# Linear attention with ELU features: first k loaded ahead of first q, new orders of issue, and rows of v, kv and z on multiples of 16 bytes

## The chip, the cores and the metric

The kernel runs on one core of a Trainium2 chip. The metric is the device time of one execution in microseconds (us). The profile is of a single execution, and its span (first to last instruction) is about 1.3 us shorter than the time of the same execution.

## The reference, cut to what matters

```python
# q, k, v: (1, 32, 2048, 128), bfloat16, normal numbers times 0.05
phi_q = jnp.where(q > 0, q + 1, jnp.exp(q)) + 1e-6
phi_k = jnp.where(k > 0, k + 1, jnp.exp(k)) + 1e-6
kv  = jnp.einsum("bhsd,bhse->bhde", phi_k, v)     # 128 x 128 a head
z   = jnp.einsum("bhsd->bhd", phi_k)
num = jnp.einsum("bhqd,bhde->bhqe", phi_q, kv)
den = jnp.einsum("bhqd,bhd->bhq", phi_q, z)[..., None] + 1e-6
return num / den
```

There are 32 heads of 2048 rows. The kernel splits phi(x) into min(exp(x), 1) + 1e-6 and max(x, 0) and gives both parts to TensorE. A column of ones beside v yields z with kv, in 129 columns.

## The kernel before

Every operation has a name and a list of operations that it waits for; a table holds the order of names on each engine. The parts that the change touches:

```python
NI, NO, NE, NR, NV, NQ, NK = 7, 12, 2, 2, 2, 2, 2      # buffers: loads, stores, em, rk, v1, q parts, kv
...
    NC = D + 1
    NW = D + 2
...
        v1_sb = sb([P, NV, NT, NW])          # rows of 130 bf16: v, a one, and one spare
        kvs_sb = sb([P, NK, NC])             # two buffers of 129 bf16
...
            # kv: 16 row blocks, each with min(exp) and with relu, all added into one place of PSUM
                    for j in range(a, b):
                        for part, src in ((0, em_sb[:, h % NE]), (1, rk_sb[:, h % NR])):
                            ins = e.matmul(kv_ps, lhsT=src[:, j], rhs=v1_sb[:, h % NV, j, 0:NC],
                                           start=(j + part == 0), stop=(j == NT - 1 and part == 1))
...
            # T: transposes of q; they overwrite what eq, rqa and rqb of the head before read
                add("PE", f"T{h}.{i}", g, over("ldq", h, ld_parts, a, b) + ["ident"] + ((every("eq", h - 1, q_parts) + rqs(h - 1)) if h else []))
...
            # n: for each of 16 row blocks the two parts of q against kv and z
                            e.matmul(to, lhsT=emq_sb[:, h % NQ, t], rhs=kvs_sb[:, h % NK], start=False, stop=False,
                                     skip_group_check=True)
                            ins = e.matmul(to, lhsT=rq_sb[:, h % NQ, t], rhs=kvs_sb[:, h % NK], start=False, stop=True,
                                           skip_group_check=True)
```

The loads (`ldq`, `ldk`, `ldv`) and stores (`st`) of 512 KB each are issued from one queue, in the order of a list. Each buffer has its own semaphore.

## Time and profile before

| | before |
|---|---|
| time, median of the first 3 runs | 170.4 us |
| span of the profiled run | 168.3 us |
| data moved | 67.12 MB |
| start of T4, from where a head takes 4.725 us | 27.48 us |
| start of T27 and of T31 (the last transposes) | 136.15 and 155.05 us |
| landing of q27, of k31, of q31 | 133.17, 148.15, 153.13 us |
| issue and landing of the last store | 165.89 and 168.30 us |

### The profile page before, as it was taken

The page shows a single profiled execution, that of the slowest core. Times are in us where ns is not written, and L with a number is a line of the kernel's source. Part 1 is how long each engine was busy: PE and PEld are TensorE (multiplying, and loading weights), DVE is VectorE, ACT ScalarE, POOL GpSimd, SP SyncE. Part 2 cuts the span into 40 slices and gives each one's busy share as a digit, 9 for nine tenths or more (in the row PEclk, how much of TensorE's full clock was granted, in tenths as well). Part 3 has the DMA queues.
Part 4 walks back from the last instruction along what each step waited for, and adds up shares of the span by engine and source line. Part 5 has one row for each costly group of instructions (what it writes and reads, how often), then busy time and mean ns, then how long its engine had stood idle before and what let it go on. Part 6 is the DMA issues. An engine that isn't in the chain of part 4 may idle for free.

```text
span 168.3 us, 6310 instructions
## 1 busy us (share of the span) xinstructions
PE 159.4 (95%) x2775; PEld 154.1 (92%) x2775; DVE 153.8 (91%) x267; ACT 153.7 (91%) x133; POOL 87.1 (52%) x71
## 2 busy tenths in 40 slices
PE   6999789999999999999999999999999999999960
PEld 2679779999999999999999999999999999999950
DVE  0177999999999999999999999999999999999894
ACT  3699989999999999999999999999999999998710
POOL 1436925556655555556555566556655565445000
PEclk9999999999999999999999999999999999999997
DMA  5999999999999999999999999999999999999986
GB/s 195 383 416 420 404 407 409 410 407 409 416 409 412 416 413 417 417 414 422 407 418 413 414 420 413 412 419 414 419 416 420 413 415 420 412 416 417 395 332 253
DMA packets 18748, 67.53 MB, mean 401 GB/s; under 512 B 2080, under 2 KB 2464, under 8 KB 18720
## 3 DMA queue, kind: packets, MB, share of 16 engines
q1 hardware_dynamic: 18720, 67.12, 98.9%
q8 instruction: 22, 0.36, 0.8%
q14 instruction: 6, 0.05, 0.1%
HBM read 50.33 MB, written 16.78 MB: 399 GB/s over the span
## 4 chain that ended last, share of the span: by engine, by line
PE 85%; DVE 8%; ACT 4%; issue 1%; POOL 0%; POOLq 0%
PE la L357 32%; PE la L394 18%; PE la L396 16%; PE la L368 16%; DVE la L410 4%; ACT la L336 2%; PE la L315 2%; DVE la L342 1%; DVE la L339 1%; ACT la L372 1%; PE la L389 1%; DVE la L403 1%; DVE la L381 1%; ACT la L378 1%; POOL la L301 0%
## 5 line engine op out<-in xcount | busy, mean ns | idle before, releaser
L410 DVE TENSOR_TENSOR la<-la 128x1536 bf16<-128x1536 f32 (+2 forms) x65 | 77.6, 1195 | 0.2
L396 PE MATMUL la<-la 128*128 128x129 bf16 x512 | 68.1, 220 | 0.0
L394 PE MATMUL la<-la 128*128 128x129 bf16 x512 | 68.0, 219 | 0.0
L372 ACT ACTIVATE la<-la 128x2048 bf16<-128x2048 bf16 (+2 forms) x35 | 60.3, 1732 | 5.7 <-PE la L368 3.8
L357 PE MATMUL la<-la 128*128 128x129 bf16 x1024 | 64.0, 219 | 0.7 <-DVE la L339 0.7
L350 POOL COPY la<-la 128x1024 int32<-128x1024 int32 (+1 forms) x33 | 41.9, 1273 | 38.1 <-DVE la L403 28.8
L336 ACT ACTIVATE la<-la 128x2048 bf16<-128x2048 bf16 (+1 forms) x33 | 61.4, 1863 | 0.0
L357 PEld LDWEIGHTS la<-la 128*128 128x128 bf16 x1024 | 60.0, 97 | 1.2 <-DVE la L339 0.8
L346 POOL TENSOR_SCALAR la<-la 128x1024 bf16<-128x1024 bf16 x32 | 44.5, 1393 | 29.1 <-DVE la L410 25.0
L396 PEld LDWEIGHTS la<-la 128*128 128x128 bf16 x512 | 49.5, 97 | 0.0
L394 PEld LDWEIGHTS la<-la 128*128 128x128 bf16 x512 | 47.1, 97 | 0.0
L368 PE MATMUL la<-la 128*128 128x128 bf16 x512 | 34.3, 221 | 0.4 <-DVE la L381 0.4
L389 PE MATMUL la<-la 128*128 128x3 bf16 (+1 forms) x192 | 32.3, 168 | 2.3 <-DVE la L410 1.6
L378 ACT ACTIVATE la<-la 128x1024 bf16<-128x1024 bf16 (+1 forms) x32 | 33.6, 1049 | 0.0
L368 PEld LDWEIGHTS la<-la 128*128 128x128 bf16 x512 | 29.9, 99 | 1.3 <-DVE la L381 0.5
L339 DVE TENSOR_SCALAR la<-la 128x2048 bf16<-128x2048 bf16 (+1 forms) x33 | 23.0, 696 | 3.6 <-ACT la L336 3.6
L389 PEld LDWEIGHTS la<-la 128*128 128x128 bf16 x192 | 18.7, 97 | 3.1 <-DVE la L410 2.0
L342 DVE TENSOR_SCALAR la<-la 128x1024 bf16<-128x1024 bf16 x32 | 17.1, 535 | 4.6 <-DMA la<-in_k_dram 4.6
L374 DVE TENSOR_SCALAR la<-la 128x2048 bf16<-128x2048 bf16 (+2 forms) x35 | 20.9, 599 | 0.3 <-ACT la L372 0.3
L381 DVE TENSOR_SCALAR la<-la 128x1024 bf16<-128x1024 bf16 x31 | 20.8, 671 | 0.0
L403 DVE RECIPROCAL la<-la 128x12 f32<-128x12 f32 (+2 forms) x65 | 12.8, 197 | 2.5 <-PE la L396 1.3
L362 ACT ACTIVATE la<-la 128x129 bf16<-128x129 f32 x32 | 9.1, 283 | 0.4 <-PE la L357 0.4
(14 smaller groups left out, 11.7 us busy)
## 6 DMA issues: line engine op xcount, KB each, us to landing
la<-in_q_dram SPq DMA_DIRECT2D x32, 512.0 KB, 15.5
la<-in_k_dram SPq DMA_DIRECT2D x32, 512.0 KB, 15.3
la<-in_v_dram SPq DMA_DIRECT2D x32, 512.0 KB, 15.3
out_dram<-la SPq DMA_DIRECT2D x31, 512.0 KB, 15.2
out_dram<-la SPq DMA_DIRECT2D x2, 192.0 KB, 2.5
out_dram<-la SPq DMA_DIRECT2D x1, 128.0 KB, 2.4
```

Source lines behind the costliest of these rows:

```text
L336: add("ACT", f"ek{h}.{i}", lambda e, a=a, b=b: e.activation(em_sb[:, h % NE, a:b], k_sb[:, h % NI, a:b], ACT.Exp), over("ldk", h, ld_parts ...
L339: add("DVE", f"em{h}.{i}", lambda e, a=a, b=b: e.tensor_scalar(em_sb[:, h % NE, a:b], em_sb[:, h % NE, a:b], 1.0, EPS, op0=ALU.min, op1=AL ...
L346: add("POOL", f"rkp{h}.{i}", lambda e, a=a, b=b: e.tensor_scalar(rk_sb[:, h % NR, a:b], k_sb[:, h % NI, a:b], BIG, 0.0, op0=ALU.min, op1=A ...
L350: add("POOL", f"v1{h}.{i}", lambda e, a=a, b=b: e.tensor_copy(v1_sb[:, h % NV, a:b, 0:D].bitcast(i32), v_sb[:, h % NI, a:b].bitcast(i32)), ...
L357: ins = e.matmul(kv_ps, lhsT=src[:, j], rhs=v1_sb[:, h % NV, j, 0:NC], start=(j + part == 0), stop=(j == NT - 1 and part == 1))
L368: ins = e.transpose(xT[:, j], q_sb[:, h % NI, j], ident[:])
L372: add("ACT", f"eq{h}.{i}", lambda e, a=a, b=b: e.activation(emq_sb[:, h % NQ, a:b], xT[:, a:b], ACT.Exp), over("T", h, t_parts, a, b) + fr ...
L378: add("ACT", f"rqa{h}", lambda e: e.activation(rq_sb[:, h % NQ, 0:n], xT[:, 0:n], ACT.Relu), over("T", h, t_parts, 0, n) + freed(NQ, h, (" ...
L389: e.matmul(_ap(o_ps[:, :], o + D, [[NC, m]]), lhsT=ones[:], rhs=epsr[:, 0:m], start=True, stop=False, skip_group_check=True)
L394: e.matmul(to, lhsT=emq_sb[:, h % NQ, t], rhs=kvs_sb[:, h % NK], start=False, stop=False, skip_group_check=True)
L396: ins = e.matmul(to, lhsT=rq_sb[:, h % NQ, t], rhs=kvs_sb[:, h % NK], start=False, stop=True, skip_group_check=True)
L410: return e.tensor_tensor(out=_ap(o_sb[:, :, :, :], first(o_sb[:, h % NO, t0, 0:1]) - first(o_sb[:, :, :, :]), [[m * D, nb], [D, m], [1, D] ...
```

## The change

The intent has two parts. First, with k loaded first, ScalarE can begin with exponentials of k, without waiting for transposes of q. The orders on all engines and of all loads and stores were drawn anew for that. Second, with rows of 272 bytes in place of 260, and buffers of 272 in place of 258, every row that TensorE streams starts at a multiple of 16 bytes.

```diff
-        w2 w1 T0.0 T0.1 w0 kv0.0 kv0.1 T1.0 n0.0 kv1.0 kv1.1 T2.0 n0.1 n1.0 kv2.0 kv2.1 T3.0 n1.1 kv3.0 kv3.1 n2.0
+        w1 w2 T0.1 T0.0 w0 T1.0 kv0.0 kv0.1 kv1.0 kv1.1 n0.0 n0.1 T2.0 kv2.0 kv2.1 n1.0 T3.0 n1.1 kv3.0 kv3.1 n2.0
 (TensorE: the rest as before; VectorE, ScalarE, GpSimd: new at both ends, VectorE in part of the middle too; cut)
-        ldq0.0 ldk0.0 ldv0.0 ldk1.0 ldq1.0 ldv1.0 ldk2.0 ldq2.0 ldk3.0 ldv2.0 ldv3.0 ldk4.0 ldq3.0 ldv4.0 ldq4.0
+        ldk0.0 ldq0.0 ldk1.0 ldv0.0 ldq1.0 ldv1.0 ldk2.0 ldk3.0 ldv2.0 ldq2.0 ldv3.0 ldq3.0 ldk4.0 ldv4.0 ldk5.0
 (queue: another order of loads and stores to the end; cut)
-    NW = D + 2
+    NW = D + 8
-        kvs_sb = sb([P, NK, NC])
+        kvs_sb = sb([P, NK, NW])
-            add("DVE", f"v1ones{s}", lambda g, s=s: g.memset(v1_sb[:, s, :, D:NW], 1.0))
+            add("DVE", f"v1ones{s}", lambda g, s=s: g.memset(v1_sb[:, s, :, D:D + 2], 1.0))
 (kvs_sb is then written and read as kvs_sb[:, h % NK, 0:NC], in three places; cut)
```

More of the change, by code (lines that the diff above doesn't have):

```diff
@@ L96 @@
     "DVE": """
-        v1ones0 rkd0.0 em0.0 eps0 em0.1 v1ones1 emq0.0 rqb0.0 emq0.1 eps1 rkd1.0 eps2 ones em1.0 r0.0 rqb1.0 f0.0
-        emq1.0 rkd2.0 em2.0 rkd3.0 em3.0 rqb2.0 r1.0 rkd4.0 r0.1 f0.1 emq2.0 f1.0 em4.0 rqb3.0 r1.1 rkd5.0 f1.1 r2.0
-        emq3.0 f2.0 em5.0 rqb4.0 r2.1 rkd6.0 f2.1 r3.0 emq4.0 f3.0 em6.0 rqb5.0 r3.1 rkd7.0 f3.1 r4.0 emq5.0 f4.0
-        em7.0 rqb6.0 r4.1 rkd8.0 f4.1 r5.0 emq6.0 f5.0 em8.0 rqb7.0 r5.1 rkd9.0 f5.1 r6.0 emq7.0 f6.0 em9.0 rqb8.0
-        r6.1 rkd10.0 f6.1 r7.0 emq8.0 f7.0 em10.0 r7.1 rqb9.0 f7.1 rkd11.0 r8.0 emq9.0 f8.0 em11.0 r8.1 rqb10.0 f8.1
@@ L102 @@
-        emq10.0 r9.0 rkd12.0 f9.0 em12.0 rqb11.0 r9.1 rkd13.0 f9.1 r10.0 emq11.0 f10.0 em13.0 r10.1 rqb12.0 f10.1
-        rkd14.0 r11.0 emq12.0 f11.0 em14.0 rqb13.0 r11.1 rkd15.0 f11.1 r12.0 emq13.0 f12.0 em15.0 r12.1 rqb14.0
-        f12.1 emq14.0 r13.0 rkd16.0 f13.0 em16.0 rqb15.0 r13.1 rkd17.0 f13.1 r14.0 emq15.0 f14.0 em17.0 rqb16.0
-        r14.1 rkd18.0 f14.1 r15.0 emq16.0 f15.0 em18.0 rqb17.0 r15.1 rkd19.0 f15.1 r16.0 emq17.0 f16.0 em19.0
-        rqb18.0 r16.1 f16.1 rkd20.0 r17.0 emq18.0 f17.0 em20.0 rqb19.0 r17.1 f17.1 rkd21.0 r18.0 emq19.0 f18.0
@@ L107 @@
-        em21.0 r18.1 rqb20.0 f18.1 rkd22.0 r19.0 emq20.0 f19.0 em22.0 r19.1 rqb21.0 f19.1 rkd23.0 r20.0 emq21.0
-        f20.0 em23.0 rqb22.0 r20.1 rkd24.0 f20.1 r21.0 emq22.0 f21.0 em24.0 rqb23.0 r21.1 rkd25.0 f21.1 r22.0
-        emq23.0 f22.0 em25.0 rqb24.0 r22.1 rkd26.0 f22.1 r23.0 emq24.0 f23.0 em26.0 rqb25.0 r23.1 rkd27.0 f23.1
-        r24.0 emq25.0 f24.0 em27.0 r24.1 rqb26.0 f24.1 r25.0 rkd28.0 emq26.0 f25.0 em28.0 r25.1 rqb27.0 f25.1
-        emq27.0 r26.0 rkd29.0 f26.0 em29.0 r26.1 rqb28.0 f26.1 emq28.0 r27.0 rkd30.0 f27.0 em30.0 rqb29.0 r27.1
@@ L112 @@
-        rkd31.0 f27.1 r28.0 emq29.0 f28.0 em31.0 r28.1 rqb30.0 f28.1 r29.0 emq30.0 f29.0 emq31.0 emq31.2 r29.1
-        emq31.1 f29.1 r30.0 f30.0 r30.1 f30.1 r31.0 f31.0 r31.1 r31.2 f31.1 f31.2
+        eps0 ones rkd0.0 v1ones1 v1ones0 eps2 rkd1.0 em0.0 rqb0.0 emq0.0 emq0.1 em0.1 em1.0 rqb1.0 rkd2.0 eps1
+        emq1.0 rkd3.0 r0.0 em2.0 f0.0 em3.0 rqb2.0 r0.1 emq2.0 f0.1 r1.0 rkd4.0 f1.0 em4.0 rqb3.0 r1.1 rkd5.0 f1.1
+        r2.0 emq3.0 f2.0 em5.0 rqb4.0 r2.1 rkd6.0 f2.1 r3.0 emq4.0 f3.0 em6.0 rqb5.0 r3.1 rkd7.0 f3.1 r4.0 emq5.0
@@ new lines @@
+        f4.0 em7.0 rqb6.0 r4.1 rkd8.0 f4.1 r5.0 emq6.0 f5.0 em8.0 rqb7.0 r5.1 rkd9.0 f5.1 r6.0 emq7.0 f6.0 em9.0
+        rqb8.0 r6.1 rkd10.0 f6.1 r7.0 emq8.0 f7.0 em10.0 rqb9.0 r7.1 rkd11.0 f7.1 r8.0 emq9.0 f8.0 em11.0 r8.1
+        rqb10.0 f8.1 emq10.0 r9.0 rkd12.0 f9.0 em12.0 r9.1 rqb11.0 f9.1 emq11.0 r10.0 rkd13.0 f10.0 em13.0 rqb12.0
+        r10.1 rkd14.0 f10.1 r11.0 emq12.0 f11.0 em14.0 rqb13.0 r11.1 rkd15.0 f11.1 r12.0 emq13.0 f12.0 em15.0
+        rqb14.0 r12.1 rkd16.0 f12.1 r13.0 emq14.0 f13.0 em16.0 rqb15.0 r13.1 rkd17.0 f13.1 r14.0 emq15.0 f14.0
@@ new lines @@
+        em17.0 rqb16.0 r14.1 rkd18.0 f14.1 r15.0 emq16.0 f15.0 em18.0 rqb17.0 r15.1 rkd19.0 f15.1 r16.0 emq17.0
+        f16.0 em19.0 rqb18.0 r16.1 f16.1 rkd20.0 r17.0 emq18.0 f17.0 em20.0 rqb19.0 r17.1 f17.1 emq19.0 r18.0
+        rkd21.0 f18.0 em21.0 r18.1 rqb20.0 f18.1 rkd22.0 r19.0 emq20.0 f19.0 em22.0 r19.1 rqb21.0 f19.1 emq21.0
+        r20.0 rkd23.0 f20.0 em23.0 r20.1 rqb22.0 f20.1 emq22.0 r21.0 rkd24.0 f21.0 em24.0 r21.1 rqb23.0 f21.1
+        emq23.0 r22.0 rkd25.0 f22.0 em25.0 rqb24.0 r22.1 rkd26.0 f22.1 r23.0 emq24.0 f23.0 em26.0 rqb25.0 r23.1
@@ L114 @@
+        rkd27.0 f23.1 r24.0 emq25.0 f24.0 em27.0 r24.1 rqb26.0 f24.1 emq26.0 r25.0 rkd28.0 f25.0 em28.0 r25.1
+        rqb27.0 f25.1 emq27.0 r26.0 rkd29.0 f26.0 em29.0 rqb28.0 r26.1 f26.1 r27.0 rkd30.0 emq28.0 f27.0 em30.0
+        rqb29.0 r27.1 rkd31.0 f27.1 r28.0 emq29.0 f28.0 em31.0 rqb30.0 r28.1 f28.1 r29.0 emq30.0 f29.0 emq31.1
+        emq31.0 r29.1 f29.1 r30.0 f30.0 r30.1 f30.1 emq31.2 r31.0 f31.0 r31.1 r31.2 f31.1 f31.2
     """,
     "ACT": """
-        eq0.0 eq0.1 ek0.0 ek0.1 rqa0 ek1.0 kvs0 eq1.0 rqa1 ek2.0 kvs1 ek3.0 eq2.0 rqa2 kvs2 ek4.0 eq3.0 kvs3 rqa3
+        ek0.0 ek0.1 eq0.1 eq0.0 rqa0 ek1.0 eq1.0 kvs0 ek2.0 rqa1 kvs1 ek3.0 eq2.0 kvs2 rqa2 ek4.0 eq3.0 kvs3 rqa3
@@ L122 @@
         ek26.0 eq25.0 kvs25 rqa25 ek27.0 eq26.0 kvs26 rqa26 ek28.0 eq27.0 kvs27 rqa27 ek29.0 eq28.0 kvs28 rqa28
-        ek30.0 eq29.0 kvs29 rqa29 ek31.0 eq30.0 kvs30 rqa30 eq31.2 eq31.0 eq31.1 kvs31 rqa31
+        ek30.0 eq29.0 kvs29 rqa29 ek31.0 eq30.0 kvs30 rqa30 eq31.1 eq31.0 kvs31 eq31.2 rqa31
     """,
     "POOL": """
-        ident0 ident rkp0.0 v10.0 v10.1 v11.0 rkp1.0 rkp2.0 v12.0 rkp3.0 v13.0 v14.0 rkp4.0 v15.0 rkp5.0 v16.0
+        ident0 ident v10.0 rkp0.0 v10.1 rkp1.0 v11.0 rkp2.0 v12.0 v13.0 rkp3.0 v14.0 rkp4.0 v15.0 rkp5.0 v16.0
         rkp6.0 v17.0 rkp7.0 v18.0 rkp8.0 v19.0 rkp9.0 v110.0 rkp10.0 v111.0 rkp11.0 v112.0 rkp12.0 v113.0 rkp13.0
@@ L132 @@
     "SP": """
-        ldq0.0 ldk0.0 ldv0.0 ldk1.0 ldq1.0 ldv1.0 ldk2.0 ldq2.0 ldk3.0 ldv2.0 ldv3.0 ldk4.0 ldq3.0 ldv4.0 ldq4.0
-        ldk5.0 ldv5.0 ldk6.0 ldq5.0 ldv6.0 ldv7.0 ldk7.0 ldq6.0 ldk8.0 ldq7.0 ldk9.0 ldk10.0 ldq8.0 ldv8.0 ldv9.0
-        ldq9.0 st0.0 ldq10.0 ldq11.0 ldq12.0 st1.0 ldv10.0 ldk11.0 ldk12.0 ldv11.0 st2.0 ldv12.0 ldq13.0 ldk13.0
-        ldv13.0 st3.0 ldk14.0 ldk15.0 st4.0 ldv14.0 ldv15.0 ldq14.0 ldk16.0 st5.0 ldk17.0 ldq15.0 ldv16.0 ldv17.0
-        st6.0 ldq16.0 ldq17.0 ldv18.0 ldk18.0 ldv19.0 ldv20.0 st7.0 ldq18.0 ldk19.0 st8.0 ldk20.0 ldk21.0 ldq19.0
-        ldk22.0 ldk23.0 st9.0 ldq20.0 ldv21.0 st10.0 ldq21.0 ldv22.0 ldk24.0 ldq22.0 st11.0 ldq23.0 ldv23.0 st12.0
-        ldv24.0 ldk25.0 ldk26.0 ldq24.0 st13.0 ldq25.0 ldv25.0 ldv26.0 st14.0 ldk27.0 ldq26.0 st15.0 ldv27.0 ldq27.0
-        ldk28.0 st16.0 ldv28.0 ldq28.0 ldk29.0 st17.0 ldv29.0 ldk30.0 ldq29.0 ldv30.0 st18.0 ldk31.0 ldq30.0 st19.0
+        ldk0.0 ldq0.0 ldk1.0 ldv0.0 ldq1.0 ldv1.0 ldk2.0 ldk3.0 ldv2.0 ldq2.0 ldv3.0 ldq3.0 ldk4.0 ldv4.0 ldk5.0
+        ldq4.0 ldv5.0 ldk6.0 ldq5.0 ldq6.0 ldv6.0 ldk7.0 ldq7.0 ldk8.0 st0.0 ldv7.0 ldv8.0 ldv9.0 ldk9.0 ldk10.0
+        ldq8.0 ldk11.0 ldq9.0 st1.0 ldv10.0 ldq10.0 ldq11.0 ldk12.0 ldk13.0 ldv11.0 ldv12.0 ldq12.0 st2.0 ldv13.0
+        ldk14.0 ldk15.0 ldv14.0 ldq13.0 ldq14.0 st3.0 ldq15.0 ldq16.0 ldk16.0 ldv15.0 ldq17.0 st4.0 ldv16.0 ldk17.0
+        ldq18.0 st5.0 ldk18.0 ldv17.0 ldk19.0 st6.0 ldv18.0 ldk20.0 ldv19.0 ldv20.0 st7.0 ldk21.0 ldq19.0 ldk22.0
+        st8.0 ldv21.0 ldq20.0 ldv22.0 st9.0 ldq21.0 ldq22.0 ldk23.0 ldk24.0 st10.0 ldv23.0 ldq23.0 st11.0 ldv24.0
+        ldk25.0 ldq24.0 st12.0 ldq25.0 ldq26.0 ldv25.0 st13.0 ldk26.0 ldv26.0 st14.0 ldk27.0 ldk28.0 ldv27.0 ldv28.0
+        st15.0 ldq27.0 ldk29.0 st16.0 ldq28.0 ldv29.0 ldq29.0 ldk30.0 st17.0 ldq30.0 ldv30.0 st18.0 ldk31.0 st19.0
         ldv31.0 ldq31.0 st20.0 st21.0 st22.0 st23.0 st24.0 st25.0 st26.0 st27.0 st28.0 st29.0 st30.0 st31.0 st31.1
@@ L361, in head @@
                     + [f"v1ones{h % NV}"] + ([f"kvs{h - 1}"] if h else []) + (fs(h - 3, [5]) if h >= 3 else []))
-            add("ACT", f"kvs{h}", lambda e: e.activation(kvs_sb[:, h % NK], kv_ps, ACT.Copy),
+            add("ACT", f"kvs{h}", lambda e: e.activation(kvs_sb[:, h % NK, 0:NC], kv_ps, ACT.Copy),
                 every("kv", h, kv_parts) + freed(NK, h, ("n", groups)))
@@ L393, in g @@
                             to = o_ps[:, o + NC * c:o + NC * (c + 1)]
-                            e.matmul(to, lhsT=emq_sb[:, h % NQ, t], rhs=kvs_sb[:, h % NK], start=False, stop=False,
+                            e.matmul(to, lhsT=emq_sb[:, h % NQ, t], rhs=kvs_sb[:, h % NK, 0:NC], start=False, stop=False,
                                      skip_group_check=True)
-                            ins = e.matmul(to, lhsT=rq_sb[:, h % NQ, t], rhs=kvs_sb[:, h % NK], start=False, stop=True,
+                            ins = e.matmul(to, lhsT=rq_sb[:, h % NQ, t], rhs=kvs_sb[:, h % NK, 0:NC], start=False, stop=True,
                                            skip_group_check=True)
```

## The prediction

> **What bounds the kernel now.** Names first. Each of 32 heads has these pieces: `ek`, `eq` (exponentials on ScalarE), `em`, `emq` (min and add on VectorE), `rkd`, `rqb` (relu on VectorE), `rkp` and `v1` (relu and copy of v on GpSimd), and on TensorE `T` (16 transposes of q), `kv` (32 matmuls into kv and z), `n` (32 matmuls for the output, in two groups n.0 and n.1). ScalarE then also has `kvs` (kv out of PSUM) and `rqa` (relu of half of q); VectorE has `r` (reciprocal) and `f` (the product that is stored). I read the page first, part by part:
>
> ```profile
> PE 159.4 (95%) x2775; PEld 154.1 (92%) x2775; DVE 153.8 (91%) x267; ACT 153.7 (91%) x133; POOL 87.1 (52%) x71
> DMA  5999999999999999999999999999999999999986
> GB/s 195 383 416 420 404 407 409 410 407 409 416 409 412 416 413 417 417 414 422 407 418 413 414 420 413 412 419 414 419 416 420 413 415 420 412 416 417 395 332 253
> q1 hardware_dynamic: 18720, 67.12, 98.9%
> ```
>
> Four resources are near full, so no share alone names the bound. Transfers: 67.12 MB at the 413 GB/s of the middle slices is 162.5 us; from the first bytes at about 2.2 us that gives 164.7, and with the last receipts some 166, against a span of 168.3. Only the last three slices show slack: 395, 332 and 253 against 413 are 259 GB/s short over 4.2 us each, 1.1 MB or 2.6 us. So **no reordering of compute can win more than about 2 us**.
>
> Then the timeline, for one steady head (ScalarE, then TensorE, whose matmuls of one kind are merged):
>
> ```profile
> 26.18 0.28 ACT L362 ACTIVATE la<-la 128x129 bf16<-128x129 f32 x1
> 26.36 1.02 ACT L378 ACTIVATE la<-la 128x1024 bf16<-128x1024 bf16 x1
> 27.26 1.91 ACT L336 ACTIVATE la<-la 128x2048 bf16<-128x2048 bf16 x1
> 29.07 1.88 ACT L372 ACTIVATE la<-la 128x2048 bf16<-128x2048 bf16 x1
> ```
> ```profile
> 24.15 2.00 PE L357 MATMUL la<-la 128*128 128x129 bf16 x32
> 25.99 0.17 PE L389 MATMUL la<-la 128*128 128x3 bf16 x1
> ...
> 27.48 1.05 PE L368 MATMUL la<-la 128*128 128x128 bf16 x16
> 28.37 0.17 PE L389 MATMUL la<-la 128*128 128x2 bf16 x1
> ```
>
> A loop closes here: kv (24.15 to 26.15) releases kvs at 26.18; kvs and rqa run to 27.38; T starts 0.10 later at 27.48, since it overwrites what rqa reads; n.1 follows at 28.37 and the next kv at 28.87. That is 4.72 us, and T comes every 4.725 us from 27.48 to 155.05. ScalarE has a reserve: its other instructions start 104 ns before the previous one's recorded end, kvs only 40 ns, so it waits about 64 ns a head.
>
> VectorE in the same stretch:
>
> ```profile
> 28.86 1.74 DVE L410 TENSOR_TENSOR la<-la 128x1536 bf16<-128x1536 f32 x1
> 30.52 0.68 DVE L339 TENSOR_SCALAR la<-la 128x2048 bf16<-128x2048 bf16 x1
> 31.11 0.68 DVE L381 TENSOR_SCALAR la<-la 128x1024 bf16<-128x1024 bf16 x1
> 31.72 0.17 DVE L403 RECIPROCAL la<-la 128x4 f32<-128x4 f32 x1
> 31.81 0.57 DVE L342 TENSOR_SCALAR la<-la 128x1024 bf16<-128x1024 bf16 x1
> 32.29 0.68 DVE L410 TENSOR_TENSOR la<-la 128x512 bf16<-128x512 f32 x1
> 32.89 0.21 DVE L403 RECIPROCAL la<-la 128x12 f32<-128x12 f32 x1
> 33.03 0.62 DVE L374 TENSOR_SCALAR la<-la 128x2048 bf16<-128x2048 bf16 x1
> 33.58 1.74 DVE L410 TENSOR_TENSOR la<-la 128x1536 bf16<-128x1536 f32 x1
> ```
>
> From f to f it is 4.72 us with no gap. So in a head with this order VectorE is as full as the loop. Where r.1 stands before rqb the trace shows a wait of about 170 ns for n.1: those heads can go faster.
>
> **What the Trainium skill says.** "SBUF — State Buffer", Specifications (TRN2): SBUF has 16-byte lines, and each access that crosses to a new line pays. The trace agrees in part. Rows of v beside ones are 260 bytes, so row j lies 0, 4, 8 or 12 bytes off a line in turn. In the single records, the first matmul on a row takes, start to start, 56.0, 60.9, 59.4 and 59.5 ns for these four, the second one on the same row 56 throughout. "TensorE: Matmul & The Clock Gate", Wait — 56ns, not 53.3ns?: N/2.4 GHz plus about 2.5 ns, an estimate of 55.8 ns for 128 columns and 56.3 for 129; the trace has 55.6 for T and 56.2 for n, and 57.5 for kv. "SBUF — State Buffer", SBUF: two separate sides: VectorE in its two-port modes and GpSimd exclude each other for whole instructions. It agrees: rkd takes 0.57 us beside GpSimd and 0.36 away from it. "DMA: Bandwidth & Descriptors", Where 436 GB/s comes from: a ceiling of 435 GB/s; the trace holds 404 to 422, so the transfers can't go faster.
>
> **Alignment.** With rows of 272 bytes every row starts on a line. Saved per head: 4 rows of each kind times (4.9 + 3.4 + 3.5) ns = 47 ns of kv. kv and z of odd heads lie 2 bytes off today: their n matmuls take 56.4 and 56.2 ns against 56.05 and 56.0 of even heads, 16 x 0.4 + 16 x 0.2 = 10 ns a head on half of the heads. The loop is 4.725 us; kv lies in it whole, so it would fall to about 4.675, for which ScalarE's 64 ns suffice. Times 31 heads: 1.5 us. But 15 of the 28 steady heads keep the VectorE order shown, 4.72 us without a gap, both before and after the change; n.0 needs the previous f.0, and has only some 0.05 us of slack there (f ends at 30.59, n.0 starts at 30.71). So these win nearly nothing, and the other 13 up to 50 ns: **0.65 us**, not 1.5. ScalarE's kvs takes the same 175 ns to the next start in either slot, so nothing there.
>
> **First k ahead of first q.** Loads land in the order of issue, 1.25 to 1.3 us apart, so I put the new order on the old landing times: k0 4.2, q0 5.4, k1 7.7, v0 9.0, q1 10.25, v1 11.5, q2 16.7, q3 19.7. ScalarE starts with ek at 4.3 instead of eq at 5.8, and is through rqa0 at 9.4 instead of 10.5. T1 now stands before kv0: T1 at 10.3, kv0 at 11.3 (before 9.35), kv1 at 13.6 behind v1's copy (before 14.1), n0 15.4 to 17.4, T2 17.4 (before 15.95), kv2 18.3 (before 20.03, where it had waited for em2, and T3 for rqb2), n1.0 20.1, rqa2 until 21.6, T3 21.7 (before 22.40), kv3 23.1, T4 26.5 against 27.48. Head: **1.0 us** won, an estimate good to 0.5. Compute alone: 1.0 + 0.65 = 1.65 us.
>
> **The transfers take most of it back.** The queue is saturated from 3 us until 159 us, so the n-th transfer lands when it did before, whatever compute does. I gave each load of the new order the landing time of its place and compared with its first use before. Most loads have 1 to 10 us to spare. Three don't: q27 moves two places back and lands at 135.73, with T27 at 136.15: 0.42 us to spare. k31 moves from place 112 to 113, lands at 149.39, and ek31 was at 150.11: 0.7 us. v31 stays at 151.88, as now just in time for GpSimd:
>
> ```profile
> 152.00 1.04 POOL L350 COPY la<-la 128x1024 int32<-128x1024 int32 x1 [1.77 <-DMA la<-in_v_dram]
> ```
>
> but its copy is needed only by kv31 at 156.45. So at T27 at most 0.4 us of the 1.5 won survives; the last four heads may add 4 x 0.05, under the 0.7 us that k31 allows: 0.6 at T31. kv31 and the last n add 0.05 to 0.1. The order of the tail (eq31 parts, one emq31 part later) I take for neutral, since the tail is kv31, n30.0, f30.0, n31, f31 as before. Sum: **0.7 us** off 170.4, that is 169.7.
>
> **Rivals.** (1) Loop alone: alignment counts in every head (1.5) and the head too (1.0): 2.5 us, cut to about 1.8 by the transfers' floor, 168.6. For it: no wait on VectorE shows on TensorE in mid-kernel today. Against: f's gapless 4.72 us and the landing of q27. (2) VectorE and transfers hide everything: 170.3. For it: q27's place; against: it has 0.4 us to spare, and the end has free bandwidth. (3) The new head is worse: kv0 starts two us later, since v0 is now fourth; if em2 or a GpSimd copy then runs late, T4 doesn't gain, and late loads cost besides: 170.8. Against: between T1 and T4 the old head loses 2.1 us to waits (16.3 us where three heads are 14.2), and these the new order largely avoids.
>
> **Range and chances.** The floor by transfers gives 168.6, the three runs of before spread by 0.5, a bad head gives 170.8. I take 168.7 to 170.5. Over 2% faster would be 167.0 or less, below the floor: 0.02. Slower by 2% needs 3.4 us of new waits: 0.01.
>
> **What would show it.** kv of a head should take 1.79 us instead of 1.84, with all first matmuls on a row at 56 ns. T4 should start near 26.5. The pitch of T should stay about 4.72 where VectorE has the gapless order and fall to 4.67 elsewhere. T27 should wait for q27's landing near 135.7, and ek31 start just behind k31. T31 should start near 154.4. It is wrong if loads land earlier by place than before (then up to 168.6), if gapless VectorE heads shorten, for instance because GpSimd's work falls elsewhere, or if the head is upset by a wait that I don't see.

## More of the kernel before

One more line of the page is needed later, the share of the engines in the chain that ended last. It is followed back from the last instruction (the last product on VectorE, not the landing of the last store), at each step to what released it:

```profile
PE 85%; DVE 8%; ACT 4%; issue 1%; POOL 0%; POOLq 0%
```

No transfer stands in it. By this chain the end is set by TensorE, and a shorter TensorE ought to help.

## The result, and the profile after

| | before | after |
|---|---|---|
| time, median of 6 runs | 170.34 us (170.03 to 170.61) | 169.93 us (169.53 to 170.39) |
| ratio, 95% interval | | 0.9977 (0.9958 to 0.9996) |
| ratio in a second session (6 runs, 11 of before) | | 0.9996 (0.9966 to 1.0026) |
| T4 | 27.48 | 27.02 |
| T26 | 131.43 | 130.50 |
| T27 | 136.15 | 136.19 |
| T31 | 155.05 | 154.99 |
| issue and landing of the last store | 165.89, 168.30 | 165.79, 168.51 |

A ratio is the mean time of one kernel's runs over that of the other's of the same rounds, so not quite the ratio of the medians. The verdict is "same": 0.4 us in the first session, and a second session that can't tell the kernels apart.

The first lines of the page, the rates of transfer by slice, and the chain that ended last, of the changed kernel:

```profile
PE 158.2 (94%) x2775; PEld 152.7 (91%) x2775; DVE 153.9 (91%) x267; ACT 153.6 (91%) x133; POOL 85.3 (51%) x71
GB/s 207 380 420 410 411 406 409 406 419 410 405 412 409 416 406 411 416 411 418 413 415 418 413 422 411 410 419 414 417 415 416 417 415 420 413 416 416 389 331 237
...
PE 76%; DMA 14%; DVE 3%; POOL 3%; SPq 1%; issue 1%
PE la L357 30%; PE la L394 17%; PE la L368 15%; PE la L396 15%; DMA la<-in_q_dram 10%; DMA la<-in_v_dram 4%; DVE la L410 3%; POOL la L350 2%; POOL la L346 1%; SPq L324 1%; PE la L389 1%; DVE la L403 0%; DVE la L374 0%
```

TensorE is busy for 1.2 us less, so matmuls did get shorter. The rates in the middle are as before, and so is the dip in the last three slices. New is that transfers hold 14% of the chain that ended last, most of it loads of q.

The timeline of one steady head on TensorE after the change (to be held against the lines of kv, n and T in the prediction):

```profile
27.02 1.05 PE L368 MATMUL la<-la 128*128 128x128 bf16 x16
...
28.41 1.98 PE L357 MATMUL la<-la 128*128 128x129 bf16 x32
30.23 0.17 PE L389 MATMUL la<-la 128*128 128x3 bf16 x1
...
31.72 1.05 PE L368 MATMUL la<-la 128*128 128x128 bf16 x16
```

From kv to the n behind it are 1.82 us instead of 1.84, and T follows T after 4.70 us instead of 4.72. Alignment is worth 25 ns a head.

Then T27, first in the kernel before, then in the changed one:

```profile
135.76 0.17 PE L389 MATMUL la<-la 128*128 128x3 bf16 x1
136.15 1.05 PE L368 MATMUL la<-la 128*128 128x128 bf16 x16
```
```profile
134.83 0.17 PE L389 MATMUL la<-la 128*128 128x3 bf16 x1
136.19 1.05 PE L368 MATMUL la<-la 128*128 128x128 bf16 x16 [0.83 <-DMA la<-in_q_dram]
```

The last part of n before T27 starts 0.93 us earlier after the change, and T27 starts 0.04 us later: it waits 0.83 us for its load of q. The pitch from T26 to T27 is 5.69 us instead of 4.70. One wait takes away all that had been won since the start.

The head of the changed kernel on TensorE and on GpSimd:

```profile
10.32 1.05 PE L368 MATMUL la<-la 128*128 128x128 bf16 x16 [0.47 <-DVE la L374]
11.22 1.98 PE L357 MATMUL la<-la 128*128 128x129 bf16 x32
14.35 1.97 PE L357 MATMUL la<-la 128*128 128x129 bf16 x32 [1.15 <-POOL la L350]
```
```profile
8.99 0.86 POOL L350 COPY la<-la 128x512 int32<-128x512 int32 x1 [7.52 <-DMA la<-in_v_dram]
9.82 1.21 POOL L346 TENSOR_SCALAR la<-la 128x1024 bf16<-128x1024 bf16 x1
10.98 0.80 POOL L350 COPY la<-la 128x512 int32<-128x512 int32 x1
11.74 1.48 POOL L346 TENSOR_SCALAR la<-la 128x1024 bf16<-128x1024 bf16 x1
13.17 1.03 POOL L350 COPY la<-la 128x1024 int32<-128x1024 int32 x1
```

T1 and kv0 start as predicted (at 10.32 and 11.22, where 10.3 and 11.3 were expected). kv1 waits for the copy of v1, which stands fifth on GpSimd and ends at 14.20. Of the four pieces ahead of it the two half copies take longer than in the old head, 0.86 and 0.80 us instead of 0.61 and 0.62; the two relus take 1.21 and 1.48, about what they took there (1.28 and 1.47).

### The profile page after: what moved, and what is told of

Its sections match the earlier page's. It is cut to its first block, busy times and chain, and to the rows that moved or that the text cites. A ratio compares the mean times of both kernels' runs of the same rounds, so it can differ in the third digit from the quotient of the medians.

```text
span 168.6 us, 6305 instructions
## 1 busy us (share of the span) xinstructions
PE 158.2 (94%) x2775; PEld 152.7 (91%) x2775; DVE 153.9 (91%) x267; ACT 153.6 (91%) x133; POOL 85.3 (51%) x71
## 3 DMA queue, kind: packets, MB, share of 16 engines
q1 hardware_dynamic: 18720, 67.12, 98.9%
## 4 chain that ended last, share of the span: by engine, by line
PE 76%; DMA 14%; DVE 3%; POOL 3%; SPq 1%; issue 1%
PE la L357 30%; PE la L394 17%; PE la L368 15%; PE la L396 15%; DMA la<-in_q_dram 10%; DMA la<-in_v_dram 4%; DVE la L410 3%; POOL la L350 2%; POOL la L346 1%; SPq L324 1%; PE la L389 1%; DVE la L403 0%; DVE la L374 0%
## 5 line engine op out<-in xcount | busy, mean ns | idle before, releaser
L350 POOL COPY la<-la 128x1024 int32<-128x1024 int32 (+1 forms) x33 | 39.9, 1209 | 46.2 <-DVE la L403 29.6
L374 DVE TENSOR_SCALAR la<-la 128x2048 bf16<-128x2048 bf16 (+2 forms) x35 | 22.4, 641 | 0.1
L381 DVE TENSOR_SCALAR la<-la 128x1024 bf16<-128x1024 bf16 x31 | 21.0, 679 | 1.5 <-ACT la L372 1.3
L342 DVE TENSOR_SCALAR la<-la 128x1024 bf16<-128x1024 bf16 x32 | 14.9, 467 | 6.5 <-DMA la<-in_k_dram 6.0
```

The lines of the kernel that those rows point to most:

```text
L350: add("POOL", f"v1{h}.{i}", lambda e, a=a, b=b: e.tensor_copy(v1_sb[:, h % NV, a:b, 0:D].bitcast(i32), v_sb[:, h % NI, a:b].bitcast(i32)), ...
```

## The experiments

Two theories stood against each other. **Q**: the place of q27 in the queue takes the gain back, so mending it gives the gain. **F**: the transfers have a floor close to the present time, so no compute shows in it. Kernels of one call ran on the same chip and share the runs of before.

**The parts apart.** `align_only` has the old orders with the new rows and buffers; `order_only` has the new orders with the old rows:

```diff
 align_only = before with
-    NW = D + 2
+    NW = D + 8          (and kvs_sb of NW, its uses cut to 0:NC; ones written into two columns only)
 order_only = after with these taken back
```

> The old orders, with only the rows of v and the buffers of kv and z on multiples of 16 bytes. Both theories: the second and third rows of kv lose their 59 to 61 ns, kv takes 1.757 us from first to last start (as in the changed kernel) and the pitch of T falls from 4.725 to 4.70, so that compute is 27 x 0.025 = 0.65 us ahead at T31. Theory Q (the place of q27 in the queue is what takes the gain back): the old load order has no such late load (the closest is q30 with 0.94 us to spare), so the time falls by 0.5 to 0.7 us, ratio 0.996 to 0.997. Theory F (the slowest of the 16 transfer engines sets the end, whatever compute does): the time falls by under 0.2 us, ratio over 0.9985.

> The new orders, with the old rows of 260 bytes and buffers of 258. Both theories: T4 near 27.0 (0.46 us earlier than before), pitch of T 4.725, T26 0.4 us earlier than before. Theory Q: T27 waits for q27 near 136.0, where compute would have been at 135.7, so the gain is gone and the time is that of before, ratio 0.999 to 1.001. Theory F: the same, ratio 0.999 to 1.001; if it shows 0.997 the gain of the change comes from the order of the transfers themselves.

`align_only`: 170.09 against 170.36, ratio 0.9989 (0.9962 to 1.0016); this interval holds what each of the two theories expected, so the time decides nothing here. kv takes 1.757 us from first to last start, as expected. At T24 compute is 0.29 us ahead (121.69 against 121.98). But T31 starts at 155.22, later than before. The loads of this execution landed later than in the trace of before, v25 at 124.19 instead of 123.00, where GpSimd had had 0.12 us to spare. GpSimd's copy and relu then fall on top of VectorE's em25, which takes 1.11 us instead of 0.68:

```profile
124.32 1.04 POOL L350 COPY la<-la 128x1024 int32<-128x1024 int32 x1 [2.67 <-DMA la<-in_v_dram]
124.79 1.11 DVE L339 TENSOR_SCALAR la<-la 128x2048 bf16<-128x2048 bf16 x1
```

T25 and T26 come after 4.86 and 5.00 us; the same happens at v31 and em31 (1.05 us). So in this execution of the old order too the lead is lost to a load, by way of GpSimd. That I had not expected.

`order_only`: 170.38, ratio 1.0 (0.9973 to 1.0028), T27 waits for q27 (landed 136.40) as expected. Wrong was T4: 27.45, no gain at all. Repeats below put the head of the new order at 27.46, 27.13 and 27.12, so against the one trace of before **the head is worth 0 to 0.5 us, not 1.0**. The old head varies as much: T4 of the other kernels with the old orders comes between 27.21 (`pitch264`) and 28.42 (`pitch512`), so single traces can't size this gain.

**The late loads mended.** In the changed kernel, q27 goes two places and k31 one place forward:

```diff
-ldv27.0 ldv28.0 st15.0 ldq27.0 ldk29.0 ... ldv30.0 st18.0 ldk31.0 st19.0
+ldv27.0 ldq27.0 ldv28.0 st15.0 ldk29.0 ... ldv30.0 ldk31.0 st18.0 st19.0
```

> The changed kernel with first-use order mended late in the queue: the load of q27 two places earlier, that of k31 one place earlier. Both theories: T27 does not wait for q27 any more, T31 starts 0.8 to 1.0 us earlier than in the changed kernel (near 154.1 instead of 155.0). Theory Q: the end follows, the time falls by 0.7 to 1.0 us against the changed kernel, ratio to before 0.991 to 0.994. Theory F: the end doesn't follow, the last store still lands near 168.3 after the first instruction, ratio to before 0.997 to 0.999.

> The changed kernel once more, on the same chip as the two runs beside it. Theory Q+F (new loads place q27 late, and the transfers' own floor lies near 169.1): ratio to before 0.996 to 0.9995; T27 waits 0.5 to 1.0 us for q27, which lands near 136.0.

> The changed kernel with q27 two places and k31 one place earlier, on the same chip as the changed kernel. Theory Q+F: no wait at T27, T31 0.5 to 0.8 us earlier, and of that 0.2 to 0.4 us shows in the time, ratio to before 0.995 to 0.998 and below that of the changed kernel. If the place of q27 doesn't matter, both ratios agree within 0.001.

T27 in `loads_early`, on TensorE's timeline, starts right behind n:

```profile
134.95 0.17 PE L389 MATMUL la<-la 128*128 128x3 bf16 x1
135.32 1.05 PE L368 MATMUL la<-la 128*128 128x128 bf16 x16
```

| | after_again | loads_early | loads_early_again |
|---|---|---|---|
| q27 landed, T27 | 135.84, 135.97 | 133.28, 135.32 | 133.15, 135.31 |
| T31 | 154.77 | 154.33 | 154.28 |
| last store issued | 165.57 | 165.24 | 165.15 |
| last store landed | 168.42 | 168.25 | 168.39 |
| ratio to before, 95% interval | 0.9996 (0.9966 to 1.0026) | 0.9967 (0.9949 to 0.9986) | 1.0006 (0.9972 to 1.0041) |

The wait is gone, and compute ends 0.4 us earlier (by the last store's issue) than in the changed kernel of the same session. The last landing moves by 0.03 us, and the time not at all. My expectation of 0.2 to 0.4 us failed in the second session. The place of q27 is what takes the lead of compute away before T27; that lead is worth nothing measurable at the end. I have no version that surely beats both kernels.

**The floor of the transfers.** `light` is the changed kernel with wrong results: the relu parts are cut to one row block and their matmuls are left out, while all 130 transfers stay in their order.

```diff
-                        for part, src in ((0, em_sb[:, h % NE]), (1, rk_sb[:, h % NR])):
+                        for part, src in ((0, em_sb[:, h % NE]),):
-                            e.matmul(to, lhsT=emq_sb[...], ...)
-                            ins = e.matmul(to, lhsT=rq_sb[...], ...)
+                            ins = e.matmul(to, lhsT=emq_sb[...], ...)
 (rqa, rqb, rkd, rkp on one block of 128 columns each)
```

> The changed kernel with wrong results on purpose: the relu parts are cut to one row block and left out of the matmuls, so that a head of compute takes about 3.9 us instead of 4.7 while every transfer stays, in the same order. It measures the floor of the transfers. Theory Q and the prediction (67.12 MB at the mean 413 GB/s): span 166 to 166.5, time 168.0 to 168.5, ratio near 0.988. Theory F: the slowest transfer engine is never idle in the changed kernel either, so the span stays 168.0 to 168.6, ratio 0.996 to 0.999.

From the page of `light`: busy time, the queue of fetched instructions, and the chain that ended last:

```profile
PE 117.8 (70%) x1751; PEld 104.7 (62%) x1751; DVE 133.3 (79%) x267; ACT 129.2 (77%) x133; POOL 54.4 (32%) x71
...
q8 instruction: 14, 0.23, 0.5%
...
DMA 56%; DVE 15%; SPq 11%; PE 9%; ACT 4%; issue 3%; POOL 1%; DVEq 0%; POOLq 0%
```

A head now takes as little as 3.9 us when nothing is missing, 0.8 us less, or 25 us over 32 heads (and this with TensorE's clock granted at 0.90 to 0.93, where the other kernels have over 0.99). The time falls by 1.2 us: 169.14 against 170.36, ratio 0.9939 (0.9915 to 0.9963). So **with far less compute the time is still 169.1: the floor lies there in this queue order, 0.5 us above the 168.6 that the prediction states**. The measured ratio lies between the two that were expected. Of 0.8 us a head, 1.2 us in all came through.

**What sets the end.** All thirteen traces answer this, at the 125th of the 130 transfers. A transfer has landed with the last of 16 raises of its semaphore (more on these below). This last raise comes at 164.44 in the kernel before, 164.69 in the changed one, and between 164.1 and 165.2 in all. In eleven traces, the kernel before and `light` among them, the last store lands 3.8 to 3.9 us after that (five stores stand behind the 125th transfer), though the last product on VectorE ends anywhere from 164.80 to 166.24. Only in `pitch288` and `pitch512`, whose last products end at 166.68 and 167.13, is it more, 4.5 and 4.9 us. So a late compute does show in the end, but an earlier one than in the kernel before only lets the last store wait longer. The last store's size and us from issue to landing, on the pages of `pitch512`, before and `light`:

```profile
out_dram<-la SPq DMA_DIRECT2D x1, 128.0 KB, 1.9
out_dram<-la SPq DMA_DIRECT2D x1, 128.0 KB, 2.4
out_dram<-la SPq DMA_DIRECT2D x1, 128.0 KB, 3.6
```

The chain on the page couldn't show this, since it starts from the last product.

**Why the floor lies higher.** A transfer's semaphore is raised 16 times, once by each of 16 transfer engines, and it has landed when the last has come. This agrees with the Trainium skill, "DMA: Bandwidth & Descriptors", Two DMAs through the same engine are not ordered: data has landed once the full increment has arrived. From the records of the raises I took, for each transfer, how far each engine lies behind the first, and the sum of the 16:

| run | sum at the 6th transfer | at the 125th | instruction fetches between | growth a fetch |
|---|---|---|---|---|
| before | 6.3 us | 46.4 us | 21 | 1.91 us |
| after | 4.1 | 42.2 | 21 | 1.81 |
| align_only | 6.8 | 45.5 | 21 | 1.84 |
| order_only | 6.8 | 46.0 | 21 | 1.87 |
| loads_early | 4.5 | 43.2 | 21 | 1.84 |
| light | 7.2 | 32.8 | 13 | 1.97 |
| light_more | 4.5 | 42.2 | 21 | 1.80 |

The six runs that are not listed have a growth of 1.72 to 1.97 us a fetch.

The fastest engine finishes a transfer every 1.253 to 1.256 us in each of these runs, `light` included: its pace doesn't depend on compute. The slowest needs 1.284 to 1.289 us and lies 5 us behind at the 125th transfer. That is why the rates dip in the last slices while landings still come every 1.25 to 1.3 us: fast engines have run out of work and the slow ones have not. Beside the data, on a queue of its own (q8), comes the program: packets of 16,384 bytes that each take 1.02 to 1.06 us in the mean of a run. They are 22 in the changed kernel and 14 in `light`, which has fewer matmuls. The Trainium skill, "Advanced Engine Details and Errata", ISA Cache, gives lines of 16 KB for 256 instructions; 5550 instructions of TensorE by 256 are 21.7, and 3502 in `light` are 13.7, so the counts agree. To test whether fetches make the engines drift, `light_more` puts the matmuls back, with the operand of their neighbour (wrong result), so that only the number of instructions and TensorE's load are again those of the changed kernel:

```diff
-                        for part, src in ((0, em_sb[:, h % NE]),):
+                        for part, src in ((0, em_sb[:, h % NE]), (1, em_sb[:, h % NE])):
 (and the second matmul of n once more with emq_sb)
```

> The light kernel with as many matmuls as the changed kernel (each one that had been left out is put back with the operand of its neighbour; the result stays wrong on purpose), other engines still light. Theory I (each fetch of 16 KB of instructions keeps one of the 16 transfer engines from its data): about 22 fetches instead of 14, and the lateness of the 16 engines against the fastest, summed at the 125th transfer, 42 to 46 us instead of 33; the fastest engine's pace stays 1.254 us for a transfer. Theory D (engines drift for other reasons, with time or bytes): the sum stays 31 to 35 us. Time between that of light (169.1) and that of before.

The page of `light_more`:

```profile
PE 157.8 (94%) x2775; PEld 152.8 (91%) x2775; DVE 135.4 (81%) x267; ACT 131.8 (78%) x133; POOL 58.3 (35%) x71
...
q8 instruction: 22, 0.36, 0.8%
...
PE 80%; DMA 12%; DVE 4%; ACT 1%; issue 0%; SPq 0%
```

There are 22 fetches again, and the sum is 42.2 us, as theory I expected. TensorE's load is back as well, so the pair alone doesn't part the two. The trace adds to it: in ten of the twelve kernels with 22 fetches the last raise falls back behind the first by 0.8 us or more between 71 and 75 us and again between 126 and 131 us, each time as a fetch runs (before: from 2.0 to 3.6 us at the fetch of 73.5, from 3.5 to 5.0 at that of 130.2). A fetch can be sized by the pair: the sum grows by 37.7 us with 21 fetches and by 25.6 with 13, an estimate of 1.5 us for each. The 1.8 to 2.0 of the table put the whole growth down to fetches; some 6 us of it must have another cause. Which engine a fetch delays the records don't tell, and 1.5 us is more than the packet's own 1.03; why stays open.

Fewer fetches did not make the slowest engine earlier in the trace of `light`: after one jump of 0.9 us it falls back slowly, without jumps, and is 5.2 us behind at the 125th transfer, where `light_more` has 4.8. What fewer fetches changed is the number of late engines (15 of 16 within 3.2 us in `light`; six at 4.5 to 4.8 in `light_more`). This profiled execution is also the slowest of the four of `light`; why the others were 0.6 to 0.8 us shorter no kept trace shows.

TensorE's pitch in `light_more` is 4.67 us, T26 starts at 128.92, 1.6 us ahead of the changed kernel, and T27 then waits until 135.71 for q27. The time is 170.71 in the median of four runs, ratio 1.0022 (0.9981 to 1.0062): **a lead of 1.6 us at T26 is worth nothing**. What `light` had won is gone; whether its few fetches or its light TensorE had won it, the runs don't part.

**What alignment does to a matmul.** The record-by-record start-to-start times of kv, averaged by row (row number mod 4), first and second matmul on the row, in ns:

| run | row 0 | row 1 | row 2 | row 3 | kv, first to last start |
|---|---|---|---|---|---|
| before (260 bytes) | 56.0, 56.3 | 60.9, 55.9 | 59.4, 55.9 | 59.5, 55.8 | 1.783 us |
| pitch264 | 56.3, 56.0 | 61.1, 55.7 | 56.1, 55.8 | 61.0, 55.6 | 1.774 |
| after (272) | 56.9, 56.5 | 56.8, 56.5 | 56.8, 56.5 | 56.8, 56.5 | 1.757 |
| pitch288 | 56.7, 56.7 | 56.7, 56.7 | 56.7, 56.7 | 56.7, 56.7 | 1.757 |
| pitch512 | 56.8, 56.5 | 56.9, 56.3 | 56.9, 56.5 | 56.9, 56.5 | 1.757 |
| same_row (272) | 56.9, 56.5 | 56.9, 56.5 | 56.9, 56.5 | 56.9, 56.4 | 1.757 |

The edits, each on the kernel `align_only`:

```diff
-    NW = D + 8
+    NW = D + 4      (pitch264)      + 16 (pitch288)      + 128 (pitch512)
-rhs=v1_sb[:, h % NV, j, 0:NC]
+rhs=v1_sb[:, h % NV, a, 0:NC]       (same_row: a is the half's first row)
```

> The old orders with rows of v beside ones of 264 bytes (so they lie 0 or 8 bytes off a line of 16 in turn) and buffers of kv and z of 264. If the start's place within 16 bytes is what costs: the first matmuls on odd rows take 59 to 60 ns and those on even rows about 56, kv from first to last start about 1.77 us. If only 4-byte or odd places cost: all rows at 56 to 57 ns.

> The old orders with rows of 288 bytes, a multiple of 32. In the aligned kernels every kv matmul takes 56.7 ns where 56.05 was expected. If places within 32 bytes matter: below 56.7, towards 56.05, kv from first to last start 1.738 us. If 16 bytes is all: 56.7 again, 1.757 us.

> The same with rows of 512 bytes. If places within 64 bytes or more matter: towards 56.05 ns, kv 1.738 us. If 16 bytes is all: 56.7 ns, 1.757 us.

> Rows of 272 bytes, and all 16 matmuls of a half of kv read the first row of that half (wrong result on purpose). If the 0.65 ns come from going to a new row every second matmul: 56.05 ns, kv 1.738 us from first to last start. If they come from the other operand or from adding 32 times into the same place of PSUM: 56.7 ns, 1.757 us.

`pitch264` (one run, 169.6 us): only rows 8 bytes off a line pay, and they pay 5 ns, once a row. So it is the place within 16 bytes. Places within 32 or 64 bytes don't matter (`pitch288`, 170.09 in one run; `pitch512`, 170.4). But no aligned kernel gets to the 56.05 ns of n: all stay at 56.7, and they stay there even when every matmul of a half reads the same row (`same_row`, result wrong, 169.44 in one run). So the 0.65 ns are not the rows'. The other operand, or 32 additions into the same place of PSUM, are left; which, no run tells. It can't be a fixed cost of each matmul: in the unaligned kernels the matmuls between the slow ones take 55.6 to 56.3 ns, with the same operands and the same place in PSUM.

## Why the prediction was right or wrong

The time, 169.93, lies in the range. That the number came so near is in part luck: the range also holds rival 2's 170.3, the floor, the saving of kv and the head were mis-sized, and T31, through which 0.6 of the 0.7 us were to come, is only 0.06 us earlier. By its steps:

- **What bounds the kernel.** Right that four resources are near full and that the transfers take back what compute wins. The floor was mis-sized: the term "67.12 MB at the 413 GB/s of the middle slices" takes the mean of 16 engines, while a transfer lands with the slowest, at 1.284 to 1.289 us a transfer where 413 GB/s makes 1.27. The working gives a span of some 166; the four spans of `light` are 167.7 to 168.5. The 168.6 stated as a time doesn't even follow from the working: 166 and the 1.3 us between span and time make 167.3. That it lies only 0.5 under the 169.1 measured is luck. Nor does "can't go faster" follow from a ceiling of 435 above slices of 404 to 422 GB/s.
- **Alignment.** The cost by row was right, and n of odd heads fell from 56.44 to 56.05 ns as expected. The saving of kv was mis-sized: 47 ns a head were expected, 26 came, because aligned matmuls run at 56.7 and not at 56.0. The pitch is 4.70, not 4.675.
- **VectorE's gapless heads.** The mechanism is there but came late. I wrote that these heads win nearly nothing. (There are 15 in each kernel, but only 12 are the same heads.) In fact most of them ran at 4.70: after the new head f of head 3 starts 5.89 us behind T4 instead of 6.10, and that lead of VectorE is used up at 20 ns a head. Only where it is spent, in four heads in a row, does T come every 4.72 us. f to f in two of them:

```profile
80.16 1.74 DVE L410 TENSOR_TENSOR la<-la 128x1536 bf16<-128x1536 f32 x1
...
84.88 1.74 DVE L410 TENSOR_TENSOR la<-la 128x1536 bf16<-128x1536 f32 x1
```

  The reading of rkd was too tidy: the 0.57 us are those that overlap GpSimd by 0.29 us, but of the twelve at 0.36 to 0.42 us five still overlap it by 0.21.

  From T4 to T26 compute won 0.47 us (0.93 at T26 less 0.46 at T4), against 0.65 over all heads: two errors that nearly cancel.
- **The head.** This step failed in size: 1.0 us expected for T4, 0.46 in the profile after and 0.02 to 0.36 in the repeats and in `order_only`. T1 and kv0 came as predicted; kv1 was put at 13.6 "behind v1's copy" and came at 14.35. The two half copies ahead of that copy took 0.43 us longer than in the old head, where VectorE was mostly idle beside them. The rest was missing in my working already: with the old head's durations for the pieces from 8.99 on, kv1 comes at about 14.0, an estimate.
- **The transfers.** Right, and the step that carried the prediction: q27 was to land at 135.73 and T27 to wait for it; it landed at 136.06 and T27 waited 0.83 us. Loads by place were right to 0.4 us in this trace and to 0.7 in `order_only`. (The list of loads without slack missed v30, which by the same table lands 0.1 us behind its first use; T31 still followed T30 after 4.70 us.) But they scatter by that much between executions, so the 0.42 us "to spare" were no gain at all here: T27 starts at 136.19 instead of 136.15, and T31 at 154.99 where 154.4 was predicted.
- **The sum.** 0.7 us were predicted; 0.4 were measured first, and 0.07 by the ratio of the second session (0.0004 of 170). Between them nothing can be told. What the predicted 0.7 assumed, that an earlier T31 brings an earlier end, is the step of the mechanism that failed: the kernel before already ended with its transfers. In `loads_early_again` T31 is 0.5 us earlier than in the changed kernel beside it and the time is the same. Where the 0.4 us of the first session came from isn't shown; the profiled execution after even lands its last store 0.21 us later than the one before.
- **Rivals.** Rival 2 (VectorE and transfers hide everything, 170.3) is nearest to what the experiments show, for the transfers' part of it.

## What to carry to other kernels

When one queue of transfers is saturated from start to end, write the landing times by place beside the times of first use, before reordering anything: compute can be no earlier than its load's place. Measure the floor by a kernel with lighter compute and the same transfers, and look at the last of the 16 raises of each semaphore, not at the mean rate. Ask also whether the last store lands later after its issue than it must: a chain that starts from the last instruction doesn't tell. Rows that TensorE streams are cheap to align to 16 bytes (3 to 5 ns for each row off a line), but that pays only where TensorE sets the end.

## What the Trainium skill lacked or had wrong

- "SBUF — State Buffer", Specifications (TRN2), gives no cost for a TensorE row that starts off a 16-byte line. Here the first matmul on such a row takes 59.4 to 61.1 ns instead of 56, the second on the same row nothing more; rows of 264 bytes pay on every second row only, and 272, 288 and 512 bytes are alike.
- "TensorE: Matmul & The Clock Gate", Wait — 56ns, not 53.3ns?: N/2.4 plus 2.5 holds for T (55.6) and n (56.05), but kv with 129 columns stays at 56.7 ns in every aligned kernel, also when all matmuls of a half read one row.
- "DMA: Bandwidth & Descriptors" doesn't say that fetches of instructions take time from transfers. Here each 16 KB fetch takes 1.02 to 1.06 us, and 8 fetches more (with TensorE's load) make the 16 engines together 12.1 us later, some 1.5 us each; after 125 transfers the slowest engine is 4.8 to 5.5 us behind the fastest in all thirteen traces, also in the one with 14 fetches.
- "Advanced Engine Details and Errata", ISA Cache, has the line of 16 KB right (22 and 14 fetches by the count of matmuls). What a fetch takes from the data of a saturated queue it doesn't say; that would also belong to "Runtime: NRT & Kernel Launch", Instruction fetch mechanics.
